# An attention and two-MoE kernel on one core: an adding DMA for the lower halves of weight sums, TensorE turns for every last token tile, no conversions on GpSimd

## The chip, the cores and the metric

The kernel runs on one core of one Trainium2 chip. The metric is the device time of one execution in microseconds (us), the median of several executions. A core has five engines that run side by side, each through its own list of instructions in a fixed order: TensorE (PE in the profile) for matrix products, VectorE (DVE), ScalarE (ACT), GpSimd (POOL) and SyncE (SP), which here only issues DMA transfers. Engines wait for one another by semaphores.

## The reference

```python
attn_out = _attn_ref(**attn_kwargs)        # softmax(q k^T / 8, causal) v ; 2 x 12 heads, 448 tokens, 64 wide
x = attn_out.transpose(0, 2, 1, 3)         # -> 896 tokens x 768
x = _moe_ref(x=x, **moe_kwargs)            # RMS norm; (silu(xn @ w_gate) * (xn @ w_val)) @ w_out ; 768 -> 1536 -> 768
return _moe2_ref(x=x, **moe2_kwargs)       # ((x @ w1) * (x @ w2)) @ w3 @ w_out ; 768 -> 1024 -> 1024 -> 768
```

All inputs and the output are float32. The kernel computes the large products to float32 accuracy.

## The kernel before

**Halves.** A float32 operand of a large product is split in two 2-byte numbers: an upper half (`hi`, float16, a rounded copy) and a lower half (`lo`, bfloat16, the rest). A product is then three TensorE products: hi x hi, hi x lo, lo x hi. `halve` makes both: `hi_part` (L441 to L444) is a copy on ScalarE (L442), with VectorE (L443) and GpSimd (L444) as other ways; `lo_part` is a subtraction on VectorE (L447) or GpSimd (L448).

**Weights.** They arrive as 8-byte numbers. `fetch` loads a tile into one of four staging tiles `st` (ring `st_r`), and VectorE (L461, L468) and ScalarE (L464, sometimes VectorE, L466) put it together as float32 in a tile `cv`. A staging tile is given out again in turn, so the load of a later weight waits until the last reader of that tile is done.

**Large products.** Gate and value (12 pieces `f`, here "gate/value"), and later w1 and w2 (8 pieces `n`, "w1/w2"), go through `wino`: a 2 x 2 scheme with seven products in place of eight. Each piece needs a `unit` of weights: two fetches of 768 columns, plain halves of three blocks, and four sums or differences of blocks, made by `sums` (L482 on VectorE, L483 on GpSimd) into the first of the unit's two staging tiles, 4 x 384 = 1536 columns, which `halve` then splits (ScalarE L442, VectorE L447). Units of gate/value have three target buffers, those of w1/w2 two. `wino` reads the seven results from PSUM by `evict` (ScalarE L815) and `join` (VectorE L818). The product with moe w_out (six pieces, "wo") is plain. The last stage ("last products") multiplies with a product of two weights that `w_prime` made earlier; its units (`funit`) have sums of 1024 columns.

**Attention.** 12 pairs of heads (`pair`): scores on TensorE, `soft` (VectorE L556, ScalarE L560), then the probabilities are halved and turned so that tokens lie on partitions. The first three row blocks (called A, one transfer for each head of the pair) and the last token tile (called B, one transfer for the pair) are turned in one of two ways. `turn` takes TensorE transposes (L596), an eviction on ScalarE (L599) and one on VectorE (L601). `send` halves first and then has SyncE issue a transposing DMA (L608). `DA` and `DB` list the pairs that use `send`: 3 to 11 for both A and B. `w_prime` (conversions of w3 and w_out, and 128 groups of products) and the first units of gate/value run beside attention. `norm` closes each batch: squares on ScalarE (L669), the reciprocal root (GpSimd L681), a product with a diagonal on TensorE, an eviction on ScalarE (L700), and for the second batch `mix`, which forms the differences that `wino` needs.

**Order.** All operations go with a priority (the numbers `TP` to `PO`), a cost and their other ways to `Plan`, which lays out one fixed list for each engine before the program is built: eight passes, forward and backward, and the best is kept. `BIAS` and `THETA` say when an operation goes to an engine that is not its first. Where TensorE would idle early in the program, the plan puts in filler products (L432), whose results nobody reads.

## Time and profile before

| | us |
|---|---|
| median of 3 executions | 550.02 (549.77 to 550.32) |
| profiled execution, its own time | 548.47 |
| span from its first to its last instruction | 546.7 |
| TensorE busy | 524.3 (96%) |
| VectorE busy | 495.8 (91%) |
| ScalarE busy | 338.8 (62%) |
| GpSimd busy | 237.5 (43%) |

The granted TensorE clock is full in every slice of the span. Matrix products are pipelined, so a busy TensorE is not one at its peak; the number to look at is how long it idles, and in which stage. Busy shares of the whole span mix stages with different limits, so they are read stage by stage: attention with `w_prime` to 168.7 us, gate/value to about 311 us, wo to 399 us, w1/w2 to about 496 us, the last products to 543 us.

### The profile page before, as it was taken

The page shows a single profiled execution, that of the slowest core. Times are in us where ns is not written, and L with a number is a line of the kernel's source. Part 1 is how long each engine was busy: PE and PEld are TensorE (multiplying, and loading weights), DVE is VectorE, ACT ScalarE, POOL GpSimd, SP SyncE. Part 2 cuts the span into 40 slices and gives each one's busy share as a digit, 9 for nine tenths or more (in the row PEclk, how much of TensorE's full clock was granted, in tenths as well). Part 3 has the DMA queues.
Part 4 walks back from the last instruction along what each step waited for, and adds up shares of the span by engine and source line. Part 5 has one row for each costly group of instructions (what it writes and reads, how often), then busy time and mean ns, then how long its engine had stood idle before and what let it go on. Part 6 is the DMA issues. An engine that isn't in the chain of part 4 may idle for free.

```text
span 546.7 us, 9215 instructions
## 1 busy us (share of the span) xinstructions
PE 524.3 (96%) x3442; PEld 286.6 (52%) x3442; DVE 495.8 (91%) x909; ACT 338.8 (62%) x492; POOL 237.5 (43%) x198
## 2 busy tenths in 40 slices
PE   6899999999899999999999999999999999999997
PEld 4565565564666554444555455555555555454553
DVE  6999999989959999999999999899658999999953
ACT  5988887896678676557464767676336553633210
POOL 4534364676453837053656420140211846673400
PEclk9999999999999999999999999999999999999999
DMA  8888799999951133334242446517104211000021
GB/s 276 288 278 263 222 252 218 258 248 184 279 112 59 34 127 130 122 109 173 70 162 78 158 172 252 208 59 236 52 0 168 65 59 59 0 1 0 35 101 68
DMA packets 55197, 77.02 MB, mean 141 GB/s; under 512 B 39792, under 2 KB 41328, under 8 KB 55152
## 3 DMA queue, kind: packets, MB, share of 16 engines
q1 hardware_dynamic: 55152, 76.43, 48.1%
q8 instruction: 27, 0.44, 0.3%
q14 instruction: 18, 0.15, 0.1%
HBM read 64.23 MB, written 2.75 MB: 123 GB/s over the span
## 4 chain that ended last, share of the span: by engine, by line
PE 54%; DVE 23%; DMA 8%; issue 5%; ACT 3%; POOL 0%; DVEq 0%; SPq 0%; ACTq 0%
PE bank L486 54%; DVE arena L818 6%; DVE arena L447 6%; DMA arena<-arena 5%; DVE cv L468 3%; DVE st L482 3%; DVE cv L461 2%; DVE arena L482 2%; DMA st<-in_wout 2%; ACT st L464 1%; DMA st<-in_w3t 1%; DVE arena L556 1%; ACT arena L442 1%; ACT arena L560 1%; DVE arena L547 0%
## 5 line engine op out<-in xcount | busy, mean ns | idle before, releaser
L486 PE MATMUL bank<-arena 128*128 128x448 f16 (+10 forms) x2976 | 446.1, 315 | 14.7 <-ACT wpr L516 3.9
L486 PEld LDWEIGHTS <-arena 128*128 128x128 f16 x3048 | 248.8, 98 | 229.0 <-issue 22.1
L464 ACT ACTIVATE st<-st 128x768 uint16<-128x768 uint16 (+2 forms) x72 | 117.6, 1658 | 32.6 <-DVE cv L461 29.9
L818 DVE TENSOR_TENSOR arena<-bank,arena 128x448 f32<-128x448 f32 x161 | 92.1, 612 | 18.1 <-PE bank L486 17.8
L442 ACT ACTIVATE arena<-arena 128x448 f16<-128x448 f32 (+2 forms) x90 | 53.9, 612 | 40.4 <-DVE arena L482 27.8
L468 DVE SCALAR_TENSOR_TENSOR cv<-st,cv 128x768 int32<-128x768 int32 (+2 forms) x84 | 75.1, 903 | 2.8 <-ACT st L464 2.6
L448 POOL TENSOR_TENSOR arena<-arena 128x448 bf16<-128x448 f32 (+2 forms) x29 | 49.6, 1713 | 56.7 <-ACT arena L442 44.5
L486 PE MATMUL bank<-xs,arena 128*128 128x448 f16 x360 | 72.4, 353 | 1.7 <-ACT arena L815 1.1
L447 DVE TENSOR_TENSOR arena<-arena 128x448 bf16<-128x448 f32 (+2 forms) x80 | 61.2, 780 | 2.4 <-ACT arena L442 1.1
L442 ACT ACTIVATE arena<-cv 128x768 f16<-128x768 f32 (+2 forms) x61 | 41.0, 679 | 32.5 <-DVE cv L468 18.6
L461 DVE TENSOR_SCALAR cv<-st 128x768 int32<-128x768 int32 (+2 forms) x84 | 50.0, 600 | 7.3 <-DMA st<-in_wout 4.2
L448 POOL TENSOR_TENSOR arena<-cv,arena 128x384 bf16<-128x384 f32 (+2 forms) x31 | 44.4, 1434 | 24.8 <-ACT arena L442 24.2
L483 POOL TENSOR_TENSOR arena<-arena 128x448 f32<-128x448 f32 x23 | 30.1, 1314 | 35.6 <-DVE arena L818 21.3
L560 ACT ACTIVATE arena<-arena 128x384 f32<-128x384 f32 (+3 forms) x84 | 41.2, 518 | 5.8 <-DVE arena L556 5.2
L444 POOL TENSOR_SCALAR arena<-cv 128x384 f16<-128x384 f32 (+2 forms) x22 | 20.2, 918 | 55.7 <-DVE cv L468 31.1
L447 DVE TENSOR_TENSOR arena<-cv,arena 128x768 bf16<-128x768 f32 (+2 forms) x53 | 43.3, 824 | 0.8 <-POOL arena L444 0.7
L447 DVE TENSOR_TENSOR arena<-st,arena 128x1536 bf16<-128x1536 f32 (+1 forms) x25 | 42.1, 1682 | 0.1
L482 DVE TENSOR_TENSOR arena<-arena 128x448 f32<-128x448 f32 x57 | 37.5, 668 | 4.1 <-ACT arena L864 4.1
L442 ACT ACTIVATE arena<-st 128x1536 f16<-128x1536 f32 (+1 forms) x22 | 30.5, 1389 | 17.4 <-DVE st L482 7.7
L556 DVE CUSTOM_DVE_ANT_0 arena<-bank,arena 128x384 f32<-128x384 f32 (+3 forms) x84 | 35.7, 441 | 1.9 <-PE bank L486 1.2
L486 PEld LDWEIGHTS bank<-arena 64*128 64x128 f32 (+2 forms) x288 | 27.5, 178 | 19.0 <-issue 5.2
L815 ACT ACTIVATE arena<-bank 128x448 f32<-128x448 f32 x23 | 12.6, 546 | 25.3 <-PE bank L486 15.2
(69 smaller groups left out, 310.2 us busy)
## 6 DMA issues: line engine op xcount, KB each, us to landing
st<-in_wgv SPq DMA_DIRECT2D x24, 768.0 KB, 4.5
st<-in_wab SPq DMA_DIRECT2D x16, 768.0 KB, 4.4
st<-in_wo SPq DMA_DIRECT2D x12, 768.0 KB, 4.4
st<-in_w3t SPq DMA_DIRECT2D x16, 512.0 KB, 4.8
st<-in_wout SPq DMA_DIRECT2D x16, 384.0 KB, 3.9
arena<-in_qk SPq DMA_DIRECT2D x12, 448.0 KB, 5.1
arena<-in_v SPq DMA_DIRECT2D x12, 256.0 KB, 3.8
out_t<-arena SPq DMA_DIRECT2D x12, 224.0 KB, 1.9
```

Source lines behind the costliest of these rows:

```text
L442: add("act", act_us(n), lambda: nc.scalar.activation(hi, src, AF.Copy), r=r, w=w, prio=prio, alt=(("dve", dve2_us(n), lambda: nc.vector.te ...
L447: add("dve", dve_us(n), lambda: nc.vector.tensor_tensor(lo, src, hi, op=ALU.subtract), r=r, w=w, prio=prio, port=True, alt=(("pool", pool_ ...
L448: port=True, alt=(("pool", pool_us(n), lambda: nc.gpsimd.tensor_tensor(lo, src, hi, op=ALU.subtract)),))
L461: add("dve", dve2_us(n), lambda: nc.vector.tensor_scalar(cv, hi, 3, 0x3FFFFFFF, op0=ALU.logical_shift_left, op1=ALU.bitwise_and), r=[ks], ...
L464: add("act", ACT_TOP * n - 0.08, lambda: nc.scalar.activation(b[:, :, 2], b[:, :, 1], AF.Copy, scale=1.0 / 8192, bias=-8191.0 / 16384), w= ...
L468: add("dve", dve_us(n), lambda: nc.vector.scalar_tensor_tensor(cv, hi, -0x3FFFFFF9, cv, op0=ALU.bitwise_and, op1=ALU.bitwise_or), r=[ks], ...
L482: add("dve", dve_us(n), lambda: nc.vector.tensor_tensor(out, a, b, op=op), port=True, alt=(("pool", pool_us(n) + 0.1, lambda: nc.gpsimd.te ...
L483: ("pool", pool_us(n) + 0.1, lambda: nc.gpsimd.tensor_tensor(out, a, b, op=op)),), **kw)
L486: nc.tensor.matmul(*a, **k)
L556: add("dve", dve_us(w), lambda: nc.vector.tensor_tensor_reduce(out=sc[:, :w], in0=ss[:, :w], in1=m, scale=-CSC, scalar=3.0e38, op0=ALU.add ...
L560: add("act", act_us(w) + 0.1, lambda: nc.scalar.activation(dst, sc[:, :w], AF.Exp, bias=mx[:, c:c + 1], scale=-1.0), r=[ksc, kmx + (c,)], ...
L818: add("dve", dve_us(S), lambda: nc.vector.tensor_tensor(dst, ps, y, op=ALU.add), r=[kp, ky], w=[kd], prio=p)
```

## The change

Five things change.

1. `halve_neg` replaces `halve` for the 1536-column sums of gate/value units 2 to 11 and of all eight w1/w2 units, and for the 1024-column sums of the six `funit`s: 24 in all. ScalarE writes the negated upper half; GpSimd issues a DMA that adds it to the float32 sums in place; ScalarE then copies the remainder, negated, to the lower half. VectorE's subtraction is gone. Both halves are now those of the negated sums, so `join` subtracts where it added (same instruction count).
2. `DB` becomes empty and `DA` 2 to 11: TensorE turns B in all 12 pairs, and pair 2 sends A by DMA.
3. GpSimd no longer makes upper halves (L444) nor the scaled copy of v (L546): these are left to ScalarE and VectorE.
4. `norm`: where values of the second norm are subtracted from earlier ones, VectorE takes them straight from PSUM (`less`); some upper and lower halves are made from PSUM (`halves`).
5. The planner's costs and the priorities are fitted anew, and fillers are put in for shorter gaps: 39 groups in place of 17.

The diff, cut to its core (the table of priorities and costs moves the order; two lines of it are shown):

```diff
-TP = 28.0521
+TP = 29.4196
...
-DA, DB = range(3,12), range(3,12)
+DA, DB = range(2,12), ()
...
             if locks:
+                us += TURN
                 t = max(t, port)
...
-LAT = {"pe": 0.25, "sp": 2.0, "dve": 0.12, "act": 0.12, "pool": 0.12}
+LAT = {"pe": 0.25, "sp": 2.4, "dve": 0.12, "act": 0.12, "pool": 0.12}
+TURN = 0.02
...
     def hi_part(n, hi, src, r, w, prio):
         add("act", act_us(n), lambda: nc.scalar.activation(hi, src, AF.Copy), r=r, w=w, prio=prio, alt=(
-            ("dve", dve2_us(n), lambda: nc.vector.tensor_copy(hi, src)),
-            ("pool", n * 0.00115 + 0.05, lambda: nc.gpsimd.tensor_scalar(hi, src, 1.0, 1.0, op0=ALU.mult, op1=ALU.mult))))
+            ("dve", dve2_us(n), lambda: nc.vector.tensor_copy(hi, src)),))
...
+    def halve_neg(n, hi, lo, src, ks, keys, prio):
+
+        add("act", act_us(n), lambda: nc.scalar.activation(hi, src, AF.Copy, scale=-1.0), r=[ks], w=keys[0], prio=prio)
+        add("pool", ISSUE, lambda: nc.gpsimd.dma_start(out=src, in_=hi, accum_op=ALU.add),
+            r=keys[0], w=[ks], prio=prio + PO["da"], port=False)
+        add("sp", accum_us(P * n * 4), lambda: None, w=[ks], prio=prio + PO["da"])
+        add("act", act_us(n), lambda: nc.scalar.activation(lo, src, AF.Copy, scale=-1.0), r=[ks], w=keys[1],
+            prio=prio + PO["da"])
...
-        ys = {}
+        ys, t1s = {}, {}
...
+            def less(dst, kd, y, ky, ps=ps, kp=kp, gc=gc):
+                add("dve", dve_us(S), lambda: nc.vector.scalar_tensor_tensor(
+                    dst, ps[:, :S], gc, y, op0=ALU.mult, op1=ALU.subtract), r=[kp, ky, "gcol"], w=[kd], prio=pr)
+
+            def halves(s, i, ps=ps, kp=kp, gc=gc, less=less):
+                (hi, kh), (lo, kl) = xs(s, i, 0), xs(s, i, 1)
+                add("act", actp_us(S), lambda: nc.scalar.activation(hi, ps[:, :S], AF.Copy, scale=gc),
+                    r=[kp, "gcol"], w=[kh], prio=pr)
+                less(lo, kl, hi, kh)
...
-        halve(1536, flat(hi[:, 3:]), flat(lo[:, 3:]), flat(s), ks, ukey(r, 3), pr)
+        (halve_neg if neg else halve)(1536, flat(hi[:, 3:]), flat(lo[:, 3:]), flat(s), ks, ukey(r, 3), pr)
...
-        halve(1024, flat(hi[:, 3:]), flat(lo[:, 3:]), flat(s), ks4, key(1), pr)
+        halve_neg(1024, flat(hi[:, 3:]), flat(lo[:, 3:]), flat(s), ks4, key(1), pr)
...
-            add("dve", dve_us(S), lambda: nc.vector.tensor_tensor(dst, ps, y, op=ALU.add), r=[kp, ky], w=[kd], prio=p)
+            add("dve", dve_us(S), lambda: nc.vector.tensor_tensor(
+                dst, *((y, ps) if minus else (ps, y)), op=ALU.subtract if minus else ALU.add), r=[kp, ky], w=[kd], prio=p)
```

The lists of the engines grow and shrink as follows (rows of the built program, equal neighbours counted once): ScalarE 422 to 509, VectorE 864 to 850, GpSimd 190 to 146, SyncE 136 to 125. Three places follow. Line numbers of the changed kernel are higher: L455 is the upper half (L442 before), L460 the lower half on GpSimd (L448), L476 the conversion in `fetch` (L464), L504 a sum on GpSimd (L483), L628 the transposing DMA (L608), L863 and L889 `evict` and the SiLU (L815, L839).

SyncE, pairs 3 and 4 of attention (before): `128x12x128` is a transfer of A for one head, `128x8x128` that of B.

```order
L608 DMA_TRANSPOSE arena<-arena 128x12x128
L608 DMA_TRANSPOSE arena<-arena 128x8x128
L608 DMA_TRANSPOSE arena<-arena 128x12x128
L459 DMA st_74<-in_wout 128x768
L538 DMA arena<-in_qk 128x896
L540 DMA arena<-in_v 128x512
L608 DMA_TRANSPOSE arena<-arena 128x12x128
L608 DMA_TRANSPOSE arena<-arena 128x8x128
L608 DMA_TRANSPOSE arena<-arena 128x12x128
```

SyncE, the same stretch of attention in the changed kernel:

```order
L628 DMA_TRANSPOSE arena<-arena 128x12x128
L471 DMA st_74<-in_wout 128x768
L628 DMA_TRANSPOSE arena<-arena 128x12x128
L561 DMA arena<-in_v 128x512
L559 DMA arena<-in_qk 128x896
L471 DMA st_71<-in_wgv 128x1536
L628 DMA_TRANSPOSE arena<-arena 128x12x128 x2
```

Two transposing transfers for each pair stand where three stood; over the whole list 20 in place of 27.

ScalarE, in the middle of gate/value (before): `128x1536` from `st` is the upper half of a unit's sums; its lower half stands on VectorE's list.

```order
L464 ACTIVATE st_73<-st_73 128x768
L442 ACTIVATE arena<-arena 128x448
L442 ACTIVATE arena<-st_71 128x1536
L839 ACTIVATE arena<-arena 128x448
L815 ACTIVATE arena<-bank_65 128x448
L442 ACTIVATE arena<-cv_77 128x768
L442 ACTIVATE arena<-cv_78 128x384
```

ScalarE, a unit of gate/value in the changed kernel: L491 is the negated upper half, L495 the lower half after the adding DMA.

```order
L476 ACTIVATE st_73<-st_73 128x768
L455 ACTIVATE arena<-arena 128x448
L491 ACTIVATE arena<-st_71 128x1536
L455 ACTIVATE arena<-cv_77 128x768
L863 ACTIVATE arena<-bank_67 128x448
L476 ACTIVATE st_72<-st_72 128x768
L889 ACTIVATE arena<-arena 128x448
L863 ACTIVATE arena<-bank_64 128x448
L491 ACTIVATE arena<-st_73 128x1536
L455 ACTIVATE arena<-cv_76 128x384
L476 ACTIVATE st_74<-st_74 128x768
L495 ACTIVATE arena<-st_71 128x1536
```

The lower half is now on ScalarE too, eight instructions behind its upper half, and it is the last reader of the staging tile `st_71`.

GpSimd, gate/value in the changed kernel: L492 is the adding DMA, between lower halves (L460) and sums (L504).

```order
L492 DMA st_73<-arena 128x1536
L460 TENSOR_TENSOR arena<-cv_76,arena 128x384
L504 TENSOR_TENSOR arena<-arena 128x448 x2
L460 TENSOR_TENSOR arena<-arena 128x448
L492 DMA st_71<-arena 128x1536
L504 TENSOR_TENSOR st_73<-cv_77,st_73 128x384
```

Ten such DMAs stand on GpSimd's list in gate/value, eight in w1/w2 and six in the last products. Of the 48 sums of gate/value units, VectorE makes 34 (before: 21) and GpSimd 14 (before: 27).

## Rows read from the trace of the kernel before

**Rows 1.** Busy us of each engine by stretch, then clock, DMA share, GB/s.

```profile
core 0: us, PE busy (x) PEld busy (x) DVE busy (x) ACT busy (x) POOL busy (x), PEclk, DMA share, GB/s
0.00:20.00 20.00, 14.18 (x98) 9.28 (x98) 14.99 (x42) 13.79 (x21) 8.90 (x24) 1.00 0.83 278
20.00:120.00 100.00, 95.57 (x906) 57.72 (x906) 93.88 (x269) 86.71 (x155) 51.95 (x52) 1.00 0.98 255
120.00:160.60 40.60, 36.66 (x433) 22.95 (x434) 33.97 (x81) 29.52 (x63) 23.38 (x19) 1.00 1.00 203
0.00:168.70 168.70, 154.50 (x1499) 97.01 (x1500) 149.14 (x400) 135.24 (x245) 85.97 (x95) 1.00 0.93 234
168.70:310.50 141.80, 137.97 (x725) 70.23 (x724) 140.37 (x201) 90.82 (x113) 74.02 (x52) 1.00 0.32 109
310.50:461.90 151.40, 151.40 (x801) 78.32 (x802) 137.41 (x203) 87.16 (x102) 46.02 (x29) 1.00 0.37 128
461.90:543.10 81.20, 80.39 (x423) 41.06 (x421) 68.35 (x109) 25.61 (x34) 31.52 (x22) 1.00 0.09 31
```

**Rows 2.** The chain that ended last: start us, us, what; transposing DMAs, then TensorE.

```profile
79.78 4.90 DMA arena<-arena
...
146.64 6.85 DMA arena<-arena
...
310.48 151.33 PE bank L486 x799
```

**Rows 3.** ScalarE's groups by shape: count, busy us, mean ns, idle before and releasers.

```profile
L442 ACT ACTIVATE arena<-cv 128x384 f16<-128x384 f32 x26 | 13.6, 524 | 8.7 <-PE bank L486 5.7 <-DVE cv L468 2.8
...
L442 ACT ACTIVATE arena<-arena 128x768 f16<-128x768 f32 x11 | 9.3, 843 | 4.5 <-DMA arena<-arena 2.9 <-issue 1.5
...
L599 ACT ACTIVATE arena<-bank 128x512 f16<-128x512 f32 x12 | 6.8, 588 | 0.4 <-PE bank L596 0.4
```

**Rows 4.** TensorE in time: one turn of four transposes; the first product of gate/value.

```profile
14.32 0.66 PE L596 MATMUL bank<-arena 128*128 128x128 f32 x4
...
168.67 3.57 PE L486 MATMUL bank<-xs,arena 128*128 128x448 f16 x18
```

**Rows 5.** Line 608, the transposing DMA: issue ns min/median/max, first and last start us.

```profile
L608 SPq DMA_TRANSPOSE arena<-arena x27: 1231/1527/4877, 69.0 to 148.0; - x27
```

**Rows 6.** VectorE's groups in gate/value (168.7 to 310.5) by shape.

```profile
L447 DVE TENSOR_TENSOR arena<-st,arena 128x1536 bf16<-128x1536 f32 x10 | 17.5, 1749 | 0.1
L461 DVE TENSOR_SCALAR cv<-st 128x768 int32<-128x768 int32 x20 | 16.6, 843 | 0.0
...
L482 DVE TENSOR_TENSOR st<-st,cv 128x384 f32<-128x384 f32 x4 | 3.6, 903 | 0.0
...
L482 DVE TENSOR_TENSOR st<-cv,cv 128x384 f32<-128x384 f32 x4 | 2.6, 646 | 0.0
```

**Rows 7.** SyncE in gate/value: who its loads waited for (us, times, longest us).

```profile
SPq L459 <- DVE arena L447: 79.1, 9, 18.5
```

**Rows 8.** One staging tile's turn in time, from its load to the next.

```profile
248.06 0.33 SPq L459 DMA_DIRECT2D st<-in_wgv  x1
...
257.22 1.32 POOL L483 TENSOR_TENSOR st<-cv 128x384 f32<-128x384 f32 x1
...
266.96 1.48 ACT L442 ACTIVATE arena<-st 128x1536 f16<-128x1536 f32 x1 [0.77 <-DVE st L482]
...
269.68 1.75 DVE L447 TENSOR_TENSOR arena<-st,arena 128x1536 bf16<-128x1536 f32 x1
...
271.45 0.33 SPq L459 DMA_DIRECT2D st<-in_wgv  x1
```

**Rows 9.** DMA issues: count, KB each, median us to landing.

```profile
st<-in_wgv SPq DMA_DIRECT2D x24, 768.0 KB, 4.5
...
out_t<-arena SPq DMA_DIRECT2D x12, 224.0 KB, 1.9
```

**Rows 10.** A small GpSimd instruction, by shape (columns as in rows 3).

```profile
L681 POOL TENSOR_TENSOR arena<-arena,mhalf 128x4 f32<-128x4 f32 x2 | 2.1, 1026 | 3.5 <-DVE arena L679 3.5
```

More of the change, by code (lines that the diff above doesn't have):

```diff
@@ L178, in schedule @@
         while done < n:
-            t, e = min((max(free[e], first[e]), e) for e in free if ready[e] and e not in idle)
+            t, e = min((max(free[e], first[e], port if e == "pool" else 0.0), e)
+                       for e in free if ready[e] and e not in idle)
             i = next((i for _, i in ready[e] if avail[i][e] <= t and not declines(t, e, i)), None)
@@ L190, in schedule @@
             if e == "pe":
-                while forward and t - free[e] > 0.5 and t < FILL and cols.get(int(free[e] / TICK), 0.0) < 1.15 * WARM:
+                while forward and t - free[e] > GAP and t < FILL and cols.get(int(free[e] / TICK), 0.0) < FULL * WARM:
                     warm.append(free[e])
@@ L267, in pool_us, with accum_us @@
     return n * 0.0019 + 0.14
+ISSUE = 0.9
+def accum_us(b):
+    return b / 460.0e3
 def dma_us(b):
-    return b / 310.0e3
+    return b / 390.0e3 + 0.1
 @with_exitstack
@@ L544, in pair @@
             r=[kvs], w=[kvh], prio=t0 + PO["vh"], alt=(
-            ("dve", dve2_us(512), lambda: nc.vector.tensor_scalar(vh[:, :, 0:D], vs, SV, 1.0, op0=ALU.mult, op1=ALU.mult)),
-            ("pool", 0.6, lambda: nc.gpsimd.tensor_scalar(vh[:, :, 0:D], vs, SV, 1.0, op0=ALU.mult, op1=ALU.mult))))
+            ("dve", dve2_us(512), lambda: nc.vector.tensor_scalar(vh[:, :, 0:D], vs, SV, 1.0, op0=ALU.mult, op1=ALU.mult)),))
         add("dve", dve_us(512), lambda: nc.vector.scalar_tensor_tensor(
@@ L615, in pair @@
             send(768, *hA_r.next(), pA[j][0], [pA[j][1] + (i,) for i in range(3)], blk[:, j * 12:j * 12 + 12],
-                 [ktA + (c, j) for c in range(3)], 1.8, t0 + PO["hA"])
+                 [ktA + (c, j) for c in range(3)], 1.9, t0 + PO["hA"])
         for c in range(0, 0 if p in DA else 12, 4):
@@ L622, in pair @@
             send(512, *hB_r.next(), pB, [kpB], tB.rearrange("p h c n -> p (h c) n")[:, :, 0:P],
-                 [ktB + (h,) for h in range(2)], 1.4, t0 + PO["hB"])
+                 [ktB + (h,) for h in range(2)], 1.8, t0 + PO["hB"])
         else:
@@ L697, in norm @@
             add("pe", 4 * S / 2400.0 + 0.03, f, r=["diag"] + [kx4 + (j,) for j in range(GH)], w=[kp], prio=pr)
+            gc = gcol[:, gi:gi + 1]
+            def less(dst, kd, y, ky, ps=ps, kp=kp, gc=gc):
[6 more added lines that the diff above has]
+                less(lo, kl, hi, kh)
+            if b and gi >= 3:
+                i = gi % 3
+                t1, k1 = t1s[i]
+                (y, ky), (y2, k2) = ys[i], (y0[gi], ("y0", gi))
+                t2, kt2 = ew_r.next()
+                halves(2, i)
+                less(y, ky, y, ky)
+                less(t2, kt2, t1, k1)
+                tt(y2, y2, t2, ALU.subtract, r=[kt2], w=[k2], prio=pr)
+                part(t1, k1, xs, 3, i, pr + PO["mx"])
+                part(y, ky, xs, 5, i, pr + PO["mx"])
+                part(t2, kt2, xs, 4, i, pr + PO["mx"])
+                part(y2, k2, xs, 6, i, pr + PO["mx"])
+                continue
             y, ky = (y0[gi], ("y0", gi)) if b == 0 else kp_r.next()
             ys[gi] = (y, ky)
-            add("act", actp_us(S), lambda y=y, ps=ps, gi=gi: nc.scalar.activation(
-                y, ps[:, :S], AF.Copy, scale=gcol[:, gi:gi + 1]), r=[kp, "gcol"], w=[ky], prio=pr)
-            if b == 0:
-                part(y, ky, xs, gi // 3, gi % 3, pr)
-            elif gi >= 3:
-                mix(xs, gi % 3, (y0[gi % 3], ("y0", gi % 3)), ys[gi % 3], (y0[gi], ("y0", gi)), ys[gi], pr)
+            if b:
+                t1s[gi] = ew_r.next()
+                less(*t1s[gi], y0[gi], ("y0", gi))
+            else:
+                halves(gi // 3, gi % 3)
+            add("act", actp_us(S), lambda y=y, ps=ps, gc=gc: nc.scalar.activation(
+                y, ps[:, :S], AF.Copy, scale=gc), r=[kp, "gcol"], w=[ky], prio=pr)
     def part(y, ky, dst, s, i, pr):
@@ L764, in ukey, with unit @@
         return [[("u", r, j, c) for c in q] for j in range(2)]
-    def unit(src, r, pr):
+    def unit(src, r, pr, neg=True):
         hi, lo = un[r]
@@ L822, in wino @@
         pr += PO["gm"]
-        join(e1, k1, *prod(4, 4, pr), e1, k1, pr)
-        join(u3, k3, *prod(5, 5, pr), e1, k1, pr)
+        join(e1, k1, *prod(4, 4, pr), e1, k1, pr, neg)
+        join(u3, k3, *prod(5, 5, pr), e1, k1, pr, neg)
         five = prod(3, 3, pr)
-        join(c22, k22, *five, u3, k3, pr)
-        join(e1, k1, *five, e1, k1, pr)
+        join(c22, k22, *five, u3, k3, pr, neg)
+        join(e1, k1, *five, e1, k1, pr, neg)
         join(c21, k21, *prod(2, 6, pr), u3, k3, pr)
-        join(e1, k1, *prod(6, 2, pr), e1, k1, pr)
+        join(e1, k1, *prod(6, 2, pr), e1, k1, pr, neg)
         return (c11, k11), (c21, k21), (e1, k1), (c22, k22)
@@ L834, in fused_kernel @@
         pr = T1 + f * step
-        unit(wgv[f], f % 3, pr + PO["g"])
-        c11, c21, c12, c22 = wino(uw(f % 3), xs, 3, pr)
+        unit(wgv[f], f % 3, pr + PO["g"], f >= 2)
+        c11, c21, c12, c22 = wino(uw(f % 3), xs, 3, pr, f >= 2)
         pr += PO["e"]
```

32 lines of the change are left out of this document (17 added, 15 removed).

## The prediction, made before the changed kernel ran

> **What bounds the kernel now.** I first read the busy times by stretch [rows 1] against the chain that ended last [rows 2]. From 168.7 us on, the end is set by TensorE: the long piece of the chain is 799 products in 151.33 us, 0.1894 us each. Gate/value has 12 x 7 x 9 products of 448 columns (pieces, products of the scheme, blocks), wo 432, w1/w2 504 and the last products 252: 1944 x 0.1894 = 368.2 us. They run from 168.67 [rows 4] to 543.0, which is 374.3 us, so only about 6 us after 168.7 are not products. In gate/value TensorE is busy 137.97 of 141.80 us (3.8 idle), beside a VectorE busy for 140.37; from 310.5 to 461.9 it never idles, and in the last stretch 0.8 us [rows 1]. What ends it is a tail of 3.7 us after the last product, which the change leaves alone.
>
> That leaves attention (0 to 168.7) and the 3.8 us. In attention TensorE idles 14.2 us [rows 1], and no engine is alone the bound: between 20 and 120 us VectorE is busy for 93.88, ScalarE for 86.71, and the DMA engines at a share of 0.98, later 1.00. The chain runs there through VectorE, ScalarE and five transposing DMAs, the first at 79.78 and the last at 146.64 us [rows 2]; each of their 27 issues holds SyncE's list 1.527 us [rows 5].
>
> **The change, part by part.**
>
> *ScalarE in attention.* In the order, up to the last pair's squares (which end at 160.6 us) ScalarE's list has 248 instructions in place of 217. Seven more upper halves of 384 columns at 0.524 are 3.7 us; four of 512 at about 0.6 are 2.5; six more of 768 at 0.843 are 5.1; one of 1536 at 1.48 [rows 3, 8]; six more evictions of a turn at 0.588 are 3.5 [rows 3]; four copies of v and two pieces of the norm at about 0.6 are 3.6; the conversions of `fetch` come out at -0.4. Sum +19.5. ScalarE was busy 13.79 + 86.71 + 29.52 = 130.0 us up to there [rows 1], and gets 149.5, of which 135.7 lie after 20 us. VectorE's list comes out even by the same count, GpSimd's gets shorter. How dense a list can ScalarE run? At its own present 0.867 (20 to 120 us) the squares end at 20 + 135.7/0.867 = 176.5, 15.9 later. At the 0.939 that VectorE reaches beside it, at 164.5, 3.9 later. Without a gap at 155.7, 4.9 earlier. I take 0.939, since VectorE's list, with as many partners, shows that a list can be kept so full there.
>
> *Transposing DMAs.* 20 in place of 27. At full share the loads of gate/value would move 109/0.32 = 341 GB/s; from 20 to 160.6 us, at full share, 100 x 255 + 40.6 x 203 = 33.7 MB were moved, which at 341 is 98.9 us of about 138.5 [rows 1]. The other 39.6 us I put down to the 27 transposes, 1.47 each; seven fewer give 10.3 us if the DMA engines are the limit. If it is SyncE's issue, each of the five pieces of the chain has one issue less ahead of it: 5 x 1.527 = 7.6. If neither, 0.
>
> *Attention together.* The stage passes from one limit to another, so I take the middle of +3.9 and -10.3: **-3.2 us**. TensorE's turns (nine more for B, three fewer for A: six at 0.66 = 4.0 [rows 4]) lie in its 14.2 idle us, and if that cover goes they cost 4.0. Fillers stand only where TensorE idles: 0. The norm is rewritten with as many steps: 0.
>
> *VectorE in gate/value.* Ten lower halves of 1536 leave it, 17.5 us; 13 sums come to it from GpSimd, at 0.646 to 0.903, mean 0.72: 9.4 us [rows 6]. It has 8 us to spare where it had 1.4. I take half of TensorE's idle 3.8: **-2.0**. Two groups of products now stand ahead of the end of the second norm; part of the -3.2.
>
> *ScalarE in gate/value and later* takes 24 remainders more (1.48 each; ten in gate/value are 15), on 90.82 busy of 141.80: covered by its idle time [rows 1]. But L495 waits for the adding DMA, and queued behind it are evictions of PSUM (L863), SiLUs and the next upper halves, for which TensorE waits.
>
> *The adding DMA* has no row. From below: the output's load of 224 KB lands in 1.9 us; from above: 768 KB land in 4.5, and this one has to read and write the sums, so twice 4.5 = 9.0 [rows 9]. It moves 768 KB of sums, so I take 4.5. Its issue holds GpSimd 0.33 (SyncE's [rows 8]) to 1.03 us (a GpSimd instruction of 4 columns [rows 10]); I take 1.0.
>
> *The staging ring.* Loads waited for the lower half on VectorE 79.1 us, nine times [rows 7]. One tile's turn, from load to load, took 271.45 - 248.06 = 23.4 us [rows 8]; in that time TensorE uses two units, 2 x 63 x 0.1894 = 23.9. The ring is at its limit. In this turn the sums, partly on GpSimd, took 257.2 to 266.9, and upper to lower half 4.4 us. After: sums on VectorE take about 5 (-4.7). Upper half 1.48, issue 1.0, DMA 4.5 and lower half 1.48 are 8.5 us, and ScalarE has eight instructions between, so I take 10 (+5.6). The turn becomes 24.3, 0.4 above the need; five turns of gate/value lose 2 us, which units ready ahead hide. **0**. At 9 us of DMA it is about 28, 4 above the need.
>
> A rule speaks against this part. The row: L461 on VectorE takes 0.843 us in gate/value [rows 6], and the trace of before has no DMA from GpSimd. The Trainium skill, SBUF — State Buffer, section "SBUF: two separate sides", says that descriptors of a DMA issued from GpSimd are written by GpSimd's cores, which are locked out while VectorE runs an operation in its two-port mode. By it up to 0.8 us would come to each adding DMA and 4 us to the sum. The Trainium skill, DMA: Bandwidth & Descriptors, section "Anatomy of one DMA — SWDGE (gpsimd) path", gives 2.0 us plus the bytes at 436 GB/s: an estimate of 3.8 us for 786 KB, by which the turn is 0.7 shorter and the sum unchanged.
>
> *w1/w2, last products.* TensorE idles 0.8 us in all there [rows 1]: nothing to gain, 0.
>
> *Sum.* 546.7 - 3.2 - 2.0 = 541.5 us of span; outside it the profiled execution had 548.47 - 546.7 = 1.77, and the median of the runs is 550.02 - 548.47 = 1.55 above the profiled one: 541.5 + 1.77 + 1.55 = **544.8**.
>
> **Rivals.**
>
> B, slower: ScalarE becomes attention's bound. For it: +19.5 us on an engine at 87%. Against it: its waits may shrink with fewer transposes. At a density of 0.90 the squares end at 170.8, +10.2; with -2.0: 558.2. It decides from a density below 0.94, where +3.1 and -2.0 give 551.1, with nothing gained from DMAs.
>
> C, slower: the adding DMA takes nearer 9 us. The turn of 28 loses about 4 us against the need, in each of nine turns of gate/value and w1/w2: 36 at most. No row shows how far units stand ready ahead; I leave a third, 13, on TensorE: 544.8 + 13 = 558. It decides from about 4 us of DMA if no unit stands ready ahead, and later the more do. For it: the ring is at its limit today [rows 7, 8].
>
> D, the change doesn't do what it says: the sums that come to VectorE, and ScalarE's longer list, eat what is relieved: 550.0.
>
> E, larger: the DMA engines were the limit of attention and ScalarE keeps up: -10.3, and gate/value's idle 3.8 goes: 546.7 - 14.1 + 3.3 = 535.9.
>
> **How the numbers follow.** Forecast (541 to 548.9) 0.39, B 0.20, C 0.14, D 0.13, E 0.14. The range leaves out most of C, some of B and the low half of E: 536 to 558. About 0.2% (548.9 to 551.1) is what a measurement of this kernel can tell from no change. Faster: forecast 0.37, E 0.14, D 0.02: 0.53. Same: D 0.10 and 0.03 of the forecast and B. Slower: B, C and D's rest, 0.34.
>
> **What would show it.** First product of gate/value near 165.5 us in place of 168.67 (B: after 175; E: 158). TensorE's idle time in gate/value near 2. VectorE there at about 133 of 140 busy. Landing of L492 at 4.5 us (C: over 7) and loads of `st` waiting for L495. No turn of TensorE longer than 0.7. It is wrong if TensorE idles behind `evict` or for lower halves after 168 us, or if ScalarE is over 95% busy in attention and the chain runs through it.

## The result, and the profile after

The changed kernel takes **558.05 us** (median of 4, 556.29 to 558.97) where the kernel before takes 550.14 on the same chip: ratio 1.0141, interval 1.0113 to 1.0168. It is 1.4% slower. The forecast was 544.8.

Busy time by stretch in the changed kernel, in the stretches of [rows 1] (the last one longer), same columns:

```profile
0.00:20.00 20.00, 17.78 (x116) 12.35 (x116) 12.63 (x36) 14.25 (x23) 5.95 (x19) 1.00 0.89 300
20.00:120.00 100.00, 94.95 (x863) 56.41 (x862) 91.17 (x258) 94.24 (x171) 28.79 (x23) 1.00 0.94 253
120.00:160.60 40.60, 38.17 (x520) 25.95 (x519) 34.47 (x100) 33.85 (x72) 20.84 (x15) 1.00 0.67 158
0.00:168.70 168.70, 159.01 (x1551) 100.59 (x1552) 143.38 (x398) 147.15 (x274) 60.20 (x61) 1.00 0.83 224
168.70:310.50 141.80, 131.85 (x695) 68.42 (x695) 128.20 (x203) 109.62 (x127) 52.64 (x44) 0.99 0.52 161
310.50:461.90 151.40, 151.40 (x802) 78.34 (x801) 120.73 (x183) 99.88 (x117) 35.54 (x29) 1.00 0.48 156
461.90:551.00 89.10, 88.39 (x467) 45.41 (x465) 66.27 (x115) 39.22 (x48) 29.61 (x27) 1.00 0.33 93
```

The row to look at is the one from 168.70 on. VectorE fell from 140.37 to 128.20 busy us of 141.80, and yet TensorE idles 9.95 us there in place of 3.8. What was taken off the busiest engine did not reach TensorE. The DMA share rose from 0.32 to 0.52.

A number that takes the stages apart is TensorE's time from the start of each product to the start of the next, summed by stage over the trace's records. Gate/value is the first 756 large products, wo the next 432, w1/w2 the next 504, the last stage 252; what lies outside them is called attention below. The two profiled executions took 548.47 and 556.29 us.

| us of TensorE's time | outside the large products | gate/value | wo | w1/w2 | last |
|---|---|---|---|---|---|
| before | 168.7 | 148.3 | 81.7 | 96.0 | 48.2 |
| changed | 169.6 | 155.7 | 81.7 | 96.0 | 47.7 |

By this count gate/value ends at 316.9 us before, not at the 311 given ahead of the prediction. 756 products at 0.1894 us are 143.2, so gate/value lost 5.1 us before and 12.5 now. The waits of TensorE over half a us in gate/value (its rows in time: start, us, in brackets the idle time before and what ended it):

```profile
194.12 1.86 PE L507 MATMUL bank<-arena 128*128 128x448 f16 x9 [1.56 <-DVE arena L867]
...
227.15 9.99 PE L507 MATMUL bank<-arena 128*128 128x448 f16 x43 [3.54 <-ACT arena L495]
...
279.07 13.81 PE L507 MATMUL bank<-arena 128*128 128x448 f16 x72 [1.08 <-DVE arena L867]
...
304.81 1.86 PE L507 MATMUL bank<-xs,arena 128*128 128x448 f16 x9 [3.39 <-ACT arena L863]
```

One is for the remainder itself (L495), one for an eviction that ScalarE came to late. The chain that ended last tells why (start, us, what; only the long pieces):

```profile
250.81 8.43 DMA st<-arena
...
259.26 1.49 ACT arena L495
...
260.77 5.96 DMA st<-in_wgv
...
277.38 7.98 DMA st<-arena
...
285.38 1.49 ACT arena L495
...
286.93 6.04 DMA st<-in_wgv
...
302.85 1.48 ACT arena L491
304.33 0.44 ACT arena L863
...
304.81 175.34 PE bank L507 x926
```

This is the staging ring: adding DMA, remainder, load of the freed tile, conversion and sums, upper half, adding DMA. Only behind the last upper half (L491) comes the eviction that TensorE waited for. Before, the chain in gate/value ran through VectorE's short pieces (L818, L447, L461, L468 and sums), a few of ScalarE's (L464) and products, and had no DMA in it, as this part of it shows:

```profile
246.36 1.67 DVE arena L447
248.03 0.48 DVE cv L461
248.53 1.93 ACT st L464
250.89 42.74 PE bank L486 x225
293.66 0.61 DVE arena L818
294.27 1.67 DVE arena L447
```

The relief of VectorE was real, and the ring took its place.

The two DMAs of that ring, issued between 200 and 310 us (count, KB each, median us to landing), first in the changed kernel, then loads before:

```profile
st<-in_wgv SPq DMA_DIRECT2D x12, 768.0 KB, 6.1
st<-arena POOLq DMA_DIRECT2D x8, 768.0 KB, 5.4
```

```profile
st<-in_wgv SPq DMA_DIRECT2D x13, 768.0 KB, 4.3
```

An adding DMA with nothing beside it landed after 4.8 us (245.56 to 250.41); the next one, with three loads beside it, after 8.4 (250.81 to 259.24). The loads took up to 8.6 us. Averaged over the first staging tiles of units 4 to 11, from records of start and end (four other kernels of the experiments are in the table already):

| mean us | load | conversion | sums | upper half | between halves | lower half | load to lower half |
|---|---|---|---|---|---|---|---|
| before | 4.5 | 7.6 | 9.2 | 1.8 | 1.9 | 1.7 | 26.7 |
| changed | 6.0 | 5.0 | 5.1 | 1.6 | 8.1 | 1.5 | 27.3 |
| x_small | 5.5 | 5.2 | 5.2 | 1.6 | 7.2 | 1.5 | 26.3 |
| x_noadd | 5.5 | 5.1 | 5.2 | 1.7 | 6.8 | 1.5 | 25.8 |
| x_halfload | 3.8 | 5.3 | 5.0 | 1.6 | 7.9 | 1.5 | 25.1 |
| x_late | 4.4 | 4.9 | 5.0 | 1.6 | 7.6 | 1.5 | 25.1 |

Sums and conversion gained 6.7 us, and the way between the halves and the loads took 7.7 back. Two units of products need 23.9. The turns differ much from one another: before, the eight took 23.3 to 33.4 us. The pace is read better from load to load of the same tile (units 4 to 10 and 5 to 11, three turns each): 26.0 us for a turn before, 27.5 in the changed kernel, 25.0 in x_late.

### The profile page after: what moved, and what is told of

Read it like the earlier page. It is cut to its first block, busy times and chain, and to the rows that moved or that the text cites. A ratio compares the mean times of both kernels' runs of the same rounds, so it can differ in the third digit from the quotient of the medians.

```text
span 554.5 us, 9401 instructions
## 1 busy us (share of the span) xinstructions
PE 530.6 (96%) x3510; PEld 292.8 (53%) x3510; DVE 459.1 (83%) x896; ACT 395.9 (71%) x563; POOL 178.0 (32%) x159
## 4 chain that ended last, share of the span: by engine, by line
PE 48%; DMA 5%; DVE 4%; ACT 2%; issue 1%; POOL 0%; DVEq 0%; POOLq 0%; SPq 0%; ACTq 0%
PE bank L507 48%; DMA st<-arena 3%; DMA st<-in_wgv 2%; DVE st L503 1%; DVE arena L459 1%; DVE cv L473 1%; ACT arena L495 1%; DVE arena L867 1%; ACT st L476 0%; DVE cv L480 0%; ACT arena L491 0%; POOL st L504 0%; DVE arena L503 0%; ACT arena L863 0%; ACT arena L455 0%
## 5 line engine op out<-in xcount | busy, mean ns | idle before, releaser
L507 PE MATMUL bank<-arena 128*128 128x448 f16 (+9 forms) x2976 | 445.5, 316 | 14.9 <-ACT arena L495 3.5
L476 ACT ACTIVATE st<-st 128x768 uint16<-128x768 uint16 (+2 forms) x76 | 122.5, 1637 | 34.7 <-DVE cv L473 34.0
L867 DVE TENSOR_TENSOR arena<-arena,bank 128x448 f32<-128x448 f32 x105 | 62.3, 611 | 15.0 <-PE bank L507 14.3
L460 POOL TENSOR_TENSOR arena<-cv,arena 128x384 bf16<-128x384 f32 (+2 forms) x34 | 45.7, 1347 | 89.1 <-ACT arena L455 82.7
L455 ACT ACTIVATE arena<-arena 128x448 f16<-128x448 f32 (+1 forms) x96 | 59.0, 625 | 18.6 <-DVE arena L503 10.0
L460 POOL TENSOR_TENSOR arena<-arena 128x448 bf16<-128x448 f32 (+1 forms) x34 | 52.3, 1545 | 56.0 <-ACT arena L455 45.4
L455 ACT ACTIVATE arena<-cv 128x384 f16<-128x384 f32 (+2 forms) x81 | 53.5, 671 | 18.4 <-PE bank L507 11.0
L473 DVE TENSOR_SCALAR cv<-st 128x768 int32<-128x768 int32 (+2 forms) x84 | 47.9, 577 | 21.5 <-DMA st<-in_wgv 8.4
L492 POOL DMA_DIRECT2D st<-arena x24 | 22.5, 962 | 131.9 <-ACT arena L491 128.6
L491 ACT ACTIVATE arena<-st 128x1536 f16<-128x1536 f32 (+1 forms) x24 | 33.0, 1376 | 23.8 <-DVE st L503 11.7
L459 DVE TENSOR_TENSOR arena<-arena 128x448 bf16<-128x448 f32 (+1 forms) x65 | 46.1, 724 | 2.3 <-ACT arena L455 2.0
L867 DVE TENSOR_TENSOR arena<-bank,arena 128x448 f32<-128x448 f32 x56 | 33.6, 614 | 16.1 <-PE bank L507 15.7
L580 ACT ACTIVATE arena<-arena 128x256 f32<-128x256 f32 (+3 forms) x84 | 41.4, 520 | 4.1 <-DVE arena L576 3.7
L459 DVE TENSOR_TENSOR arena<-cv,arena 128x384 bf16<-128x384 f32 (+2 forms) x50 | 42.0, 844 | 0.3
L504 POOL TENSOR_TENSOR arena<-arena 128x448 f32<-128x448 f32 x21 | 26.8, 1281 | 41.9 <-DVE arena L867 27.8
L495 ACT ACTIVATE arena<-st 128x1536 bf16<-128x1536 f32 (+1 forms) x24 | 32.9, 1375 | 7.0 <-DMA st<-arena 7.0
L576 DVE CUSTOM_DVE_ANT_0 arena<-bank,arena 128x256 f32<-128x256 f32 (+3 forms) x84 | 35.8, 444 | 1.0 <-ACT arena L580 0.3
L503 DVE TENSOR_TENSOR arena<-arena 128x448 f32<-128x448 f32 x50 | 33.4, 678 | 2.2 <-ACT arena L914 2.2
```

The lines of the kernel that those rows point to most:

```text
L455: add("act", act_us(n), lambda: nc.scalar.activation(hi, src, AF.Copy), r=r, w=w, prio=prio, alt=(("dve", dve2_us(n), lambda: nc.vector.te ...
L459: add("dve", dve_us(n), lambda: nc.vector.tensor_tensor(lo, src, hi, op=ALU.subtract), r=r, w=w, prio=prio, port=True, alt=(("pool", pool_ ...
L460: port=True, alt=(("pool", pool_us(n), lambda: nc.gpsimd.tensor_tensor(lo, src, hi, op=ALU.subtract)),))
L473: add("dve", dve2_us(n), lambda: nc.vector.tensor_scalar(cv, hi, 3, 0x3FFFFFFF, op0=ALU.logical_shift_left, op1=ALU.bitwise_and), r=[ks], ...
L476: add("act", ACT_TOP * n - 0.08, lambda: nc.scalar.activation(b[:, :, 2], b[:, :, 1], AF.Copy, scale=1.0 / 8192, bias=-8191.0 / 16384), w= ...
L495: add("act", act_us(n), lambda: nc.scalar.activation(lo, src, AF.Copy, scale=-1.0), r=[ks], w=keys[1], prio=prio + PO["da"])
```

## The experiments

Two kinds of kernel were run. In the first, all lists keep the order of the changed kernel and one thing is altered in place; in the second, code is altered and the planner lays out every list anew. Ratios are to the kernel before on the same chip (changed: 1.0141).

### First round: is it the adding DMA, and what does undoing it give?

**x_noadd**, same order:

```diff
-nc.gpsimd.dma_start(out=src, in_=hi, accum_op=ALU.add)
+None
```

> The changed kernel with every list in the same order, but the 24 adding DMAs are left out (so the lower halves of the sums are wrong). Theory R (ring): the loss lies in gate/value, because a staging tile's turn is now some 26 to 30 us where TensorE needs 23.9, and the adding DMA (4.8 us alone, 6 to 8.8 beside loads) is on that turn. Then the turn falls under 23.9, TensorE's idle time in gate/value falls from about 10 to 4 us or less, and the time to 548 to 552. Theory S (ScalarE's longer list in attention and its place ahead of evictions): nothing of that changes, 555 to 558.

548.92 us, 0.9977 (0.9952 to 1.0002). TensorE's time in gate/value is 148.2, 7.5 less than in the changed kernel. Theory R holds, theory S falls. But with lower halves that cost neither VectorE nor a DMA anything, the kernel is only level with the one before.

**x_plain**, laid out anew: `halve` in place of `halve_neg` everywhere.

> The changed kernel with the lower halves of all 24 sums by VectorE's subtraction again; everything else of the change stays, the order is laid out anew. Theory R: gate/value idles about as before the change (4 to 5 us), the rest of the change is worth about +1, so 549 to 552. Theory S or a loss by the refitted order: 555 to 558.

560.9, 1.0205 (1.015 to 1.026): neither theory. Attention is 175.3, gate/value 151.2.

**b_neg**, laid out anew: the kernel before, with `halve_neg` as in the change.

> The kernel before with part 1 alone (negated halves and adding DMAs), its own priorities and ways, the order laid out anew. Theory R: gate/value loses some 6 to 10 us, 555 to 560. Theory S: ScalarE's list in attention is unchanged, so 548 to 551.

571.64, 1.0386 (1.0341 to 1.0432): gate/value 164.4, w1/w2 102.5. The sign fits R, the size is over it.

**x_r31**, laid out anew: in `unit`, first halves take three staging tiles in turn, second halves the fourth.

> The changed kernel with the four staging tiles given out otherwise for units: three in turn for the first half of a unit (which then holds the sums), one for every second half; the order is laid out anew. Theory R: a tile that holds sums has three units of time (35.9 us) in place of two (23.9), the wait for the lower half leaves the loads' queue, gate/value idles under 4 us: 548 to 552, unless the one tile for second halves (4.3 to 6 us of load and some 5 of conversion against 11.9 for a unit) becomes the limit. Theory S: 555 to 558.

565.1, 1.0261 (1.0219 to 1.0303): gate/value 161.5. Four tiles in turn were better than three and one, or the layout was worse for another reason; this can't be told. All three new layouts came out slower than either kernel, so from here on what had to tell causes apart kept the order.

### Second round: what in the DMA, and could another engine do it?

**x_small**, same order: `out=src[:, :32], in_=hi[:, :32]` in the adding DMA.

> The changed kernel with every list in the same order, but each adding DMA moves 32 columns in place of 1536 or 1024 (lower halves of the others are wrong): GpSimd's issue and the fixed part of a DMA stay, the bytes go. Without the DMAs the time was 548.9, with them 558.1. If the bytes on the DMA engines, beside the loads, make the loss: 549 to 551. If issue, queueing on GpSimd's list and the fixed part make it: 554 to 557.

554.13, 1.0092 (1.0065 to 1.012), gate/value 152.9: the second range. Of the 1.6% between all bytes and no DMA, the bytes are 0.5%, and a DMA that moves nearly nothing but is waited for is 1.1%. It landed after 2.3 us (median, 200 to 310 us); but of these eight, the three issued within 0.6 us of a load took 4.0 to 5.2 us and landed 0.16 us after that load, the other five 2.0 to 2.6. So a part of the 1.1% may again be the meeting with loads, which the small size does not take away. The Trainium skill, DMA: Bandwidth & Descriptors, section "Anatomy of one DMA — SWDGE (gpsimd) path", has 2.0 us as the fixed part; the trace agrees, with 2.0 to 2.1 for the shortest of these. For 786 KB its fit gives an estimate of 3.8; measured are 4.8 alone, and the measured number stands.

**x_vlo**, same order: no DMA, and in L495's place

```diff
-nc.scalar.activation(lo, src, AF.Copy, scale=-1.0)
+nc.vector.scalar_tensor_tensor(lo, src, -1.0, hi, op0=ALU.mult, op1=ALU.subtract)
```

> The changed kernel with every list in the same order, but no adding DMAs; in place of ScalarE's remainder VectorE computes the negated lower half, at the same place in the program (1.75 us each, 24 times). The result is the reference's. Theory R (the adding DMA's way on the ring makes the loss): 548 to 552, as without the DMA, since VectorE's 126 busy us of 140 in gate/value become some 144 on 137 needed, less what contention with GpSimd falls away. Rival V (VectorE is the bound of gate/value as soon as it takes the halves back): 556 or more.

569.92, 1.039 (1.0362 to 1.0418): rival V. Its stretch from 170 to 310 us:

```profile
170.00:310.00 140.00, 130.52 (x677) 67.13 (x676) 137.33 (x207) 95.06 (x115) 52.01 (x34) 0.98 0.32 109
```

VectorE is at 137.33 of 140 again, and TensorE idles 9.5. Gate/value took 157.2 us, and w1/w2 106.7 in place of 96.0, so most of what this kernel loses against the changed one lies in w1/w2, where VectorE was busy for 88.88 of 90 us from 430 us on. In this order, with sums moved to VectorE, it has no room for the halves: the adding DMA is not a loss against that, and a comparison with "VectorE does it" depends on the layout around it.

**x_hip**, same order: every second upper half of `w_prime` by `nc.gpsimd.tensor_scalar(hi, w, 1.0, 1.0, ...)` in its place.

> The changed kernel with every list in the same order, but 16 of the 32 upper halves of w_prime go to GpSimd at the places that ScalarE had them (part 3 half undone): some 9 us less of ScalarE's work in attention. Theory S (ScalarE, 113.6 busy of 120 us, is the bound of attention): gate/value starts 3 to 8 us earlier, 550 to 555. Otherwise (gate/value alone makes the loss) 557 to 560.

559.86, 1.0199 (1.0173 to 1.0225). ScalarE has 16 instructions less in attention and is busy for 135.2 us up to 160.6 in place of 142.3, and attention took 171.3, not less than the 169.6 of the changed kernel: the length of ScalarE's work was not its bound.

**x_nofill**, same order: `pl.order(lambda: None)`.

> The changed kernel with every list in the same order, but the 39 groups of fillers left out. If they stand only in idle time and do nothing for the clock: 557.5 to 558.5. If some stand on the path: 550 to 556. If they keep the granted clock at full: a granted clock well under 1 in the first 50 us and 560 or more.

559.65, 1.018 (1.0146 to 1.0214). Its first stretches:

```profile
0.00:20.00 20.00, 12.98 (x49) 6.74 (x49) 13.59 (x36) 14.53 (x24) 5.76 (x19) 0.68 0.88 296
20.00:40.00 20.00, 17.64 (x109) 10.21 (x109) 15.64 (x35) 18.25 (x28) 3.39 (x3) 0.81 0.84 282
```

The granted clock is 0.68 in the first 20 us (a mix of the 1.2 and 2.4 GHz levels), in which TensorE is busy for 12.98; with the fillers it was 1.00, and TensorE busy for 17.78. The first product of gate/value comes at 175.03 in place of 167.00, 8 us later, gate/value took 152.4 in place of 155.7, and by the medians the whole is some 2 us longer (0.4%, and the intervals of the two kernels overlap). So gate/value takes back a part of lost attention time, 3.3 of 8 us in this trace.

### Third round: other ways through the ring

**x_plo**, same order: GpSimd's `tensor_tensor(lo, src, hi, op=ALU.subtract)` in place of the DMA, no remainder, plain signs.

> The changed kernel with the other lists' order held, but GpSimd computes the 24 lower halves itself, by a subtraction in the place where it issued the adding DMA; ScalarE's remainder is gone. The result is the reference's. Theory R (upper to lower half on the staging ring, 8.1 us between them and 1.5 for the remainder in the changed kernel, makes the loss): a subtraction of 3 to 4 us takes the turn of 27.3 below 23.9, 547 to 552. Rival V (VectorE, which GpSimd's long subtractions hold up, becomes the bound): 556 to 566.

578.34, 1.0496 (1.0464 to 1.0528): rival V, gate/value 165.4, w1/w2 106.7. GpSimd's subtractions took 3.1 to 3.7 us each in gate/value, and VectorE was nearly full without having got any work:

```profile
170.00:310.00 140.00, 125.46 (x644) 64.27 (x643) 133.66 (x187) 90.85 (x110) 71.96 (x41) 0.96 0.27 102
```

VectorE's own instructions took longer: L473 on 768 columns 1042 ns in the mean from 165 to 320 us, against 658 in the changed kernel.

**x_near**, same order but for L495: its start in the plan is taken 2.5 us earlier when lists are written out.

> The changed kernel with the adding DMAs, but ScalarE's 24 remainders (L495) stand up to 2.5 us of the plan earlier in its list; all other lists are the same. In half of the units the remainder began 2 to 5 us after the DMA had landed. Theory R: 1 to 2 us of each turn come off, 554 to 557. Rival: ScalarE then waits for DMAs, evictions behind it come late, 558 to 561.

570.54, 1.0372 (1.0338 to 1.0406): the rival, and more. What ScalarE waited for ahead of its remainders (us, times), in the changed kernel and here:

```profile
  DMA st<-arena: 7.0, 4
```

```profile
  DMA st<-arena: 43.3, 15
```

ScalarE stood 43.3 us for DMAs, with evictions and upper halves behind. A wait on a list holds up all that is queued behind it; the eight instructions between the halves were the cover.

**x_abf**, laid out anew: `neg` false in gate/value. **x_db**, laid out anew: `DA, DB = range(3,12), range(3,12)`.

> The change with part 1 in w1/w2 and the last products alone; units of gate/value have VectorE's lower halves again, the order is laid out anew. If the loss of the changed kernel is that of adding DMAs in gate/value: 549 to 553. The kernel with no adding DMA at all took 560.9; if VectorE's list in gate/value is what costs there, 558 to 563.

> The change with part 2 undone (pairs 3 to 11 send A and B by DMA, as before), the order laid out anew. Attention takes 169.6 us of TensorE's time in the changed kernel, 168.7 before. If part 2 is worth what the prediction took (7.6 to 10.3 us, covered by the ring of gate/value or by ScalarE): 560 or more. If it is worth nothing: 555 to 559.

x_abf: 556.53, 1.0114 (1.0084 to 1.0143), in neither range; gate/value 152.9, attention 173.5. x_db: 569.03, 1.0342 (1.0315 to 1.0369); attention 174.0, gate/value 163.0. x_db lost 7 us in a stage that its edit doesn't touch, so neither says what its part is worth.

### Fourth round: time on the ring or issue, and the planner's costs

**x_issue**, same order: the DMA of 32 columns goes to a tile `scrap` (cleared once, at the start). **x_noadd_near**: x_noadd with remainders 5 us earlier. **x_cost**, laid out anew: `accum_us` b / 160.0e3, `dma_us` b / 250.0e3. **x_halfload**, same order, for units from the fifth on:

```diff
-out=st, in_=src.bitcast(I32).rearrange("p (n t) -> p n t", t=2)
+out=st[:, :n // 2], in_=src.bitcast(I32).rearrange("p (n t) -> p n t", t=2)[:, :n // 2]
```

> The changed kernel, all lists in the same order; GpSimd still issues 24 adding DMAs, of 32 columns, into a scratch tile that nobody reads, so that ScalarE's remainder waits for none (lower halves wrong). Against the kernel before on the same chip: without any adding DMA the ratio was 0.998, with 32 columns that are waited for 1.009, with all of them 1.014. If what costs is the time from issue to landing on the staging ring: 0.996 to 1.001 (547 to 550.5). If it is the issue on GpSimd's list, which VectorE or the order feels: 1.006 to 1.010 (553 to 555.5).

> As the kernel without adding DMAs (548.9), and the 24 remainders stand up to 5 us of the plan earlier in ScalarE's list, closer behind the upper halves; lower halves wrong. Theory R: the eight other instructions that the list keeps between the halves (6.8 us without a DMA) are on the staging ring as well; 2 to 4 us less in each turn bring gate/value's time from 148.2 to 144 to 147 us and the whole to 544 to 548. Rival: the ring is then no limit any more, 548 to 550.

> The changed kernel, all lists in the same order, with adding DMAs; the loads of gate/value's units 4 to 11 bring half of the columns (weights wrong): the DMA engines have half the bytes beside the adding DMAs, and a load itself is shorter by some 2 us. Theory R with contention: load (6.0 us) and upper to lower half (8.1) get shorter by 3 to 4 us together, gate/value loses 5 to 7 us less, 550 to 553. If the ring doesn't set the pace: 557 to 559.

> The changed kernel with the planner's two DMA costs at measured size (adding DMA 4.9 us of transfer in place of 1.7, loads 3.1 in place of 2.1), everything else the same, order laid out anew. If the loss comes from an order that was laid out for adding DMAs that are too short: 546 to 554. If the adding DMA loses whatever the order: 556 to 565.

- x_issue: 549.99, 1.0002 (0.9974 to 1.0031). Issued but not waited for, the DMA costs next to nothing (0.25% against x_noadd, the intervals overlap; its profiled run, the longest of ten at 553.9, had 150.5 in gate/value). It is the way from issue to landing that costs.
- x_halfload: 548.22, 0.9965 (0.9944 to 0.9986), gate/value 146.8, with all adding DMAs in place. These landed hardly sooner (median 5.4 as before, still up to 8.8), and the way between the halves stayed at 7.9; what got shorter is the load, 3.8 in place of 6.0. So the lever is the whole turn of the ring, and a shorter load takes back as much as leaving out the adding DMA.
- x_noadd_near: 552.1, 1.0038 (1.0016 to 1.0061): no gain, rather a loss against x_noadd, though the way between the halves fell to 2.6 and the turn to 24.9; the rest of the ring was no limit any more.
- x_cost: 580.48, 1.0555 (1.0522 to 1.0588), gate/value 169.3, attention 176.2. True prices for two operations did not make a better layout.

### Fifth round: the same bytes at another time

**x_late**, complete; ScalarE, VectorE, GpSimd and TensorE keep their lists, on SyncE's list eight loads change place:

```diff
+    for u in range(6, 12):
+        pl.behind[gv0 + 2 * u + 1] = gv0 + 2 * (u // 2 * 2 - 1)
+    for x in (1, 3):
+        pl.behind[len(pl.loads) + x] = gv0 + 2 * 11
```

> The changed kernel, complete and with the adding DMAs; the lists of TensorE, VectorE, ScalarE and GpSimd are the same, and on SyncE's list alone the loads of the second halves of units 6 to 11 and two early loads of wo, which are needed 14 to 30 us after their issue, stand behind the loads of the first halves, which are converted as soon as they land. Theory R with contention: the first halves land in 4.3 to 5 us in place of 6.0, adding DMAs meet fewer loads (5 us in place of up to 8.8), 2 to 4 us less in each turn of the ring, and the loss of gate/value goes as it went with half loads (548.2): 547 to 551. If contention between loads and adding DMAs is not the point: 556 to 559.

549.77 (12 runs), 0.9991 (0.997 to 1.0012): 1.5% faster than the changed kernel, level with the one before. Gate/value took 146.7 us, 9.0 less than in the changed kernel and 1.6 less than before; attention took 172.1 in this run. Loads and adding DMAs from 200 to 310 us:

```profile
st<-in_wgv SPq DMA_DIRECT2D x14, 768.0 KB, 5.2
...
st<-arena POOLq DMA_DIRECT2D x8, 768.0 KB, 4.9
```

The first halves alone, which the ring waits for, took 4.4 us in the mean in place of 6.0. The landings of adding DMAs from 240 to 310 us (us min/median/max), changed and x_late:

```profile
DMA to landing us min/median/max: 4.8/6.4/8.8
```

```profile
DMA to landing us min/median/max: 4.8/4.9/8.8
```

And the stretch from 170 to 300 us, changed and x_late:

```profile
170.00:300.00 130.00, 123.44 (x648) 63.74 (x647) 116.60 (x185) 98.94 (x115) 47.52 (x40) 0.99 0.50 158
```

```profile
170.00:300.00 130.00, 127.14 (x680) 66.63 (x678) 125.09 (x197) 106.39 (x125) 52.28 (x44) 1.00 0.53 167
```

The DMA share is no lower (0.53 against 0.50); TensorE is busy 3.7 us more. So it is shown that the loss hung on loads, not yet needed, that stood on SyncE's list ahead of needed ones: unit 6's second half was loaded at 197.5 us and first used at 219.1, and unit 4's first half, issued at 201.2 behind it, was awaited on landing at 207.4. Two things got shorter together, the needed loads (6.0 to 4.4) and the landings of two adding DMAs (8.4 and 8.0 to 4.9 us). No run takes them apart in full, but x_halfload, in which little but the load got shorter, gained as much; and without any adding DMA the loads still took 5.5 (x_noadd), so of their rise from 4.5 to 6.0 the larger part comes from other loads.

**x_late_notr**, x_late without its 20 transposing DMAs:

> The kernel with the loads behind (549.8), all lists in the same order, without its 20 transposing DMAs: the turned probabilities of pairs 2 to 11 are left as pairs 0 and 1 made them (attention's result wrong). It tests the other missed term, attention, where 7.6 to 10.3 us were forecast from seven transposes fewer and TensorE's time outside the large products stayed at 169.6 to 172 (168.7 before). If transposes, as DMA time or as waits of the chain, are a limit of attention: all 20 away bring it down by 5 us or more, 540 to 545. If they are not: 547 to 550, and attention stays within 2 us.

545.25, 0.9931 (0.9905 to 0.9957), just above the lower range: 0.6% or 3.3 us under x_late. From 20 to 140 us, x_late and x_late_notr:

```profile
20.00:140.00 120.00, 112.69 (x1117) 68.70 (x1115) 107.63 (x311) 111.75 (x208) 38.91 (x31) 1.00 0.87 234
```

```profile
20.00:140.00 120.00, 115.09 (x1169) 70.74 (x1168) 109.33 (x322) 113.21 (x214) 41.40 (x32) 1.00 0.56 184
```

The DMA share falls by a third, TensorE gains 2.4 us of 120, attention 5.6 in the two traces (172.1 to 166.5), with gate/value unchanged at 146.7. Transposes are a limit among others: 0.2 to 0.3 us each.

## Why the prediction was wrong

**What bounds the kernel** was right: TensorE from 168.7 us on, losses in gate/value, none in wo. The measured time lies on rivals C (558, at 0.14) and B (558.2), not on the forecast (0.39). By stage, the forecast had -2.0 for gate/value and -3.2 for attention; measured are +7.4 and +0.9.

**The staging ring: the step that failed.** The turn was put at 24.3 us, 0.4 above the need, which units ready ahead would hide, so 0 for TensorE. It was 27.3 in the mean, and gate/value took 7.4 us more.

- The base was wrong. The 23.4 us of today's turn were one tile's, nearly the shortest of eight; their mean is 26.7. The ring was not at its limit but over it. From load to load a turn took 1.5 us more than before, where 0.9 was forecast; five turns of 1.5 are an estimate of 7.5, about what gate/value lost. "Which units ready ahead hide" had no row, and that was noted for rival C but not for the sum; nothing shows that any of it was hidden.
- The terms: the adding DMA was priced at 4.5 and takes 4.8 with nothing beside it, near enough, but up to 8.8 beside loads, 6.3 in the mean of units 4 to 11 (upper through lower half: 11.2 against 10 assumed). The load was left at its old 4.2 and took 6.0. The saving of 4.7 on sums was 4.1, and conversion saved 2.6 besides, which was not foreseen.
- What was left out: both DMAs of the ring run beside each other and beside other loads, loads start close together (227.12 and 227.69 us, 254.94 and 256.50), and SyncE's list had early loads ahead of urgent ones. The prediction looked at a duration, not at what runs beside it. Of the signs it named, TensorE idled 9.95 us in gate/value where near 2 stood, and behind `evict` and a lower half; L492 landed after 5.4 us in the median, between its 4.5 and rival C's 7.

Rival C had about the turn (28), for a wrong reason: a DMA that is slow by itself. That its 13 us match the 13.3 by which the forecast was missed is luck: it had them all in the turns of gate/value and w1/w2, where gate/value was 9.4 off and w1/w2 lost nothing (96.0 both times); 4.1 came from attention. Rival B met the time too, but not its sign: the squares ended at 161.1, not 170.8.

**Attention: second failure.** -3.2 was forecast; TensorE's time outside the large products went from 168.7 to 169.6 (other runs of the same order: 169.9 to 172.3). The first product of gate/value did come earlier, at 167.00, but products of the second norm stand behind it.

- ScalarE's term came near by two errors against each other: its work up to 160.6 grew by 12.3 us, to 14.25 + 94.24 + 33.85 = 142.3, where +19.5 was counted, and it was busy for 0.911 of the time from 20 us on, where 0.939 was taken. The last squares end at 161.1 where 164.5 was forecast. x_hip shows that this length was no bound.
- The term for transposes was mis-sized: 10.3 us for seven if the DMA engines are the limit; all 20 in x_late_notr are worth 3.3 us by the medians and 5.6 by the traces, seven so 1.2 to 2. A DMA share near 1.00 beside busy compute engines was read as a bound; at 0.56 the stage was hardly faster.

**VectorE in gate/value: -2.0** did not come in the changed kernel, nor in x_noadd, which is level with before without any cost of lower halves. In x_late, with the loads put in order, gate/value was 1.6 us shorter than before, so about this size may have been there behind the ring.

**Covers** held in wo, w1/w2 and the last products. Fillers stand on no path (x_nofill is no faster), and they keep the clock up, which was not said. TensorE was busy for 150.90 us up to 160.6 in place of 146.41; that the turns among this cost nothing is not shown, since no run takes them away. The Trainium skill, SBUF — State Buffer, section "SBUF: two separate sides", would have a DMA from GpSimd wait while VectorE runs an operation in its two-port mode. In gate/value issues of adding DMAs took 0.88 us in the median, and landings without loads beside 4.8 to 4.9 each time, so the traces have no sign of 0.8 us more for some of them; no run was made to test it.

**What stays open.** What each part of the change is worth in a layout of its own: new layouts moved stages that an edit doesn't touch by several us. Why attention did not shorten by the 1 to 2 us that seven transposes should give. And whether the kernel before would gain from its loads in another order too: x_late was not tried on it, so nothing here shows the adding DMA to be worth more than what it replaced.

## What to carry to other kernels

When work goes from a busy engine to a DMA, list every transfer that will run beside it and who waits for that one: a price without company is a lower bound. On an in-order queue of loads, put the load that is used on landing ahead of those that are used 20 us later; here eight places on one list were worth 1.5%. Where a planner lays out all lists anew, test a cause with the order held; undoing a part and laying out again measures the layout.

## What was not expected of the hardware

- Four loads of 768 KB issued within 4.1 us landed after 4.3, 5.9, 6.2 and 8.6 us, where one by itself takes 4.2: one issued early delays one needed soon.
- An adding DMA within on-chip memory, 768 KB of sums, takes 4.8 us alone, not far from a load's 4.2; 512 KB take 3.9 to 4.6 (5.5 just behind another adding DMA), 16 KB 2.0 to 2.6. It does not pay twice for reading and writing. But small size does not help beside a load: three of 16 KB, issued within 0.6 us of a load of 768 KB, took 4.0 to 5.2 us and landed just after it (x_small).
- Kernels whose order in attention is the same differ there by up to 2.7 us between profiles (169.6 to 172.3 outside the large products), so a difference of 1 us in a single profile says nothing.
